# TensorE in the emitted order: alternating heads, feed-forward by column budget, maxima by halves

## The chip, the cores and the metric

One core of one Trainium2 chip runs the whole program. The metric is device time in microseconds (us) of one execution. Below, PE is TensorE (matmuls), PEld its weight loads, DVE is VectorE, ACT is ScalarE, POOL is GpSimd, and SP issues most of the DMAs.

## The reference, cut to what matters

Attention whose queries and keys are hashed to six bits, and which counts a key only where both hashes agree; then a gated feed-forward block over the heads' joined outputs. Four batches, eight heads, 768 rows, 64 columns a head.

```python
mask = q_bucket[:, :, :, None] == k_bucket[:, :, None, :]
scores = np.where(mask, scale * np.matmul(q, k.transpose(0, 1, 3, 2)), -1e9)
attn = np.exp(scores - np.max(scores, axis=-1, keepdims=True))
x = np.matmul(attn / (np.sum(attn, axis=-1, keepdims=True) + 1e-09), v)   # heads side by side: 512
u, w = np.split(np.maximum(x @ w_in, 0.0), 2, axis=-1)                    # 1024 wide
w = (w - mean(w)) / np.sqrt(var(w) + 1e-06)
out = (u * (np.einsum('ts,bsd->btd', w_spatial, w) + b_spatial[None, :, None])) @ w_out
```

## The kernel before, in words

Two heads make a pair: head 0 lies on partitions 0 to 63, head 1 on 64 to 127. There are 16 pairs, four a batch, and the rows are taken 128 at a time, so the attention has 96 steps; step g is row tile i = g % 6 of pair p = g // 6.

**A step.** `scores` (L269) fills one PSUM tile of two banks for each head (pool `ps_sc`, two tiles in all), by `sums` (L221): four passes of products, each as two column halves of 384 for each of the two heads, 16 matmuls. Operands are fp16 numbers split in a high and a low part, and the last pass adds the mask. The program's loops name the two heads in turn: `for a in passes, for c in halves, for e in heads`. A head's matmul uses only its 64 (or 63) rows of the array.

For most pairs, DVE then takes each row's extreme from the score tile (L285), ACT the exponential (L286) and a cast to fp16 (L293), DVE or POOL the low part (L294), and one transposing DMA on SP's queue turns the result (`pt<-pp`, L296). Three steps later (`LAG`) `weighted` multiplies it with V, 18 matmuls for each head (L309 to L311, "pv").

For pairs 1, 2 and 3 (`KEYS`) keys stand on the rows, so nothing needs to be turned: ACT takes the exponential (L277), and one step later 6 fp32 matmuls for each head follow (L266). These pairs need the rows' maxima beforehand: `row_max` (L236) makes a row tile's sums again, 8 matmuls, into two tiles of `ps_sc`, and DVE reduces them (L243). After six row tiles the maxima go to one line (a transpose on PE, L254, and a small DMA to `hk`).

**The feed-forward block.** When a batch's four pairs are done, 28 units stand in a queue: `v_unit`, `u_unit`, `s_unit`, `o_unit`, each 12 or 18 matmuls of 384 or 512 columns into one bank of `ps_m` (two banks, used by hashes and mean rows too). They run beside the next batch's attention; the last batch's run at the end, a part of them beforehand (`partial_units`).

**What sets the order.** `at(g, k)` gives each instruction a priority. A scheduler, which holds a model of the engines, places the instructions of all engines by it and by when it thinks their inputs are there. It so decides PE's order too: which head's matmul is next, where a unit falls between the scores of a step. Each engine then works off its list. Units are dropped into the program by whole units, `credit += 28.0 / STEPS` a step.

Also beside the first batch, `weights_gen` (L103) turns the feed-forward weights from 64 bits to fp16 pairs, 36 jobs; those of `w_in` and `w_out` have four DVE instructions each (L138 to L141).

Of the kernel before, what the change touches and what calls it, by code (L numbers as in the profile page):

```python
# [36 lines left out]
def lsh_attention_spatial_gating(  # L37
# [183 lines left out]
    def sums(p, ps, rows, passes, queries):  # L221

        for a, (x, y, last) in enumerate(passes):
            for c in range(2):
                cs = slice(c * HS, (c + 1) * HS)
                for e in range(2):
# [3 lines left out]
                    nc.tensor.matmul(ps[e][:, c], lhsT=f(l)[:, rows], rhs=f(m)[:, cs],  # L230
# [5 lines left out]
    def row_max(p, i):  # L236
        ps = [ps_sc.tile([P, 2, 512], F32, tag="sc", name=f"mp{p}_{i}_{e}")[:, :, :HS] for e in range(2)]
        sums(p, ps, slice(i * P, (i + 1) * P), ALL[2:], (True, True))
        for e in range(2):
            n = 2 * p + e  # L240
            if i == 0:
                st["mx", n] = wk.tile([P, NT], F32, tag="mx", bufs=3, name=f"mx{n}")
            nc.vector.reduce_max(st["mx", n][:, i:i + 1], ps[e], axis=AX.XY)  # L243
        if i < NT - 1:
            return
        for e in range(2):
            n = 2 * p + e
            nb = st["nb", n] = wk.tile([P, NT], F32, tag="nb", bufs=6, name=f"nb{n}")
            mx = st.pop(("mx", n))
            m16 = wk.tile([P, NT], F16, tag="m16", bufs=2, name=f"m16_{n}")  # L250
            nc.vector.tensor_scalar(m16, mx, -float(2 ** 27), -1.0 / HK, op0=ALU.max, op1=ALU.mult)
            nc.gpsimd.tensor_scalar(nb, mx, -ISQ, None, op0=ALU.mult)
            tp = ps_m.tile([P, 512], F32, tag=MT, name=f"tp{n}").bitcast(F16)
            nc.tensor.transpose(out=tp[0:NT, 0:P], in_=m16, identity=ident)  # L254
# [90 lines left out]
    def partial_units():  # L345
# [7 lines left out]
        def unit(name, lhs, rhs, dst):  # L353
            ps = ps_m.tile([P, 512], F32, tag=MT, name=name)[:, :dst.shape[-1]]
            k = 0
            for c in range(NPAIR - 1):
                for t in THREE:
                    nc.tensor.matmul(ps, lhsT=lhs(c, t), rhs=rhs(c, t), start=(k == 0), stop=(k == 3 * NPAIR - 4))  # L358
                    k += 1
            nc.scalar.copy(dst, ps)  # L360

        def v_part(i):
            flat = vb[i // 3].rearrange("p a s -> p (a s)").bitcast(F32)
            dst = st["vpart", i] = flat[:, (i % 3) * F2:(i % 3 + 1) * F2]
            unit(f"vpp{i}", lambda c, t: xt[c][:, t[0], i * P:(i + 1) * P], lambda c, t: wi[t[1]][:, c, F2:DF], dst)

        def u_part(d):
            dst = st["upart", d] = ub[:, d]
            unit(f"upp{d}", lambda c, t: wi[t[0]][:, c, d * P:(d + 1) * P], lambda c, t: xt[c][:, t[1], 0:HS], dst)
# [3 lines left out]
    def mlp_units(b):  # L373
# [14 lines left out]
        def v_unit(i):  # L388
# [3 lines left out]
            for c in range(k0 // 3, NPAIR):  # L392
                for gx, gw in THREE:
                    nc.tensor.matmul(ps, lhsT=xt[c][:, gx, i * P:(i + 1) * P], rhs=wi[gw][:, c, F2:DF],  # L394
# [12 lines left out]
            if i % 3 == 2:  # L407
                norm(i // 3)

# [20 lines left out]
        def u_unit(d, h):  # L430
# [10 lines left out]
            for c in range(k0 // 3, NPAIR):  # L441
                for gw, gx in THREE:
                    nc.tensor.matmul(ps[:, :HS], lhsT=wi[gw][:, c, d * P:(d + 1) * P], rhs=xt[c][:, gx, hs],  # L443
# [6 lines left out]
            nc.scalar.activation(u[h][:, d], ps, AF.Relu, scale=1.0 / SX)  # L450

        gt = {}

        def s_unit(d, h):
# [5 lines left out]
            for c in range(NT):  # L460
                for gv, gw in THREE:
                    nc.tensor.matmul(ps[:, :HS], lhsT=vn[gv][:, c, d * P:(d + 1) * P], rhs=ws[gw][:, c, hs],  # L462
# [6 lines left out]
            nc.gpsimd.tensor_tensor(out=gt[h][1][:, d], in0=y, in1=gt[h][0][:, d], op=ALU.subtract)  # L469

        def o_unit(i):
# [3 lines left out]
            for c in range(NF):  # L475
                for gg, gw in THREE:
                    nc.tensor.matmul(ps, lhsT=gt[h][gg][:, c, j * P:(j + 1) * P], rhs=wo[gw][:, c, :],  # L477
# [4 lines left out]
            nc.sync.dma_start(out=out[b, i * P:(i + 1) * P, :], in_=o)  # L482

# [34 lines left out]
    G_W = 0  # L518
    G_U = 1
    STEPS = NPAIR * NT  # L520
    LASTB = (NP - NPAIR) * NT + LAG
    LRATE = 1.48
    HQS = (nc.sync, nc.scalar, nc.gpsimd)
# [4 lines left out]

    at(-40, 0)
# [8 lines left out]
    queue = []  # L538
    wdone = 0
    credit = 0.0  # L540
    wv = 0
    rml = [(NT * p + i - LEAD, p, i) for p in sorted(KEYS) for i in range(NT)]
# [109 lines left out]
```

## Time and profile before

| | us |
|---|---|
| median of 3 runs (lowest, highest) | 897.3 (890.99, 898.1) |
| the profiled execution | 894.64 |
| its span, first to last instruction | 892.9 |
| PE busy in it | 829.5 |
| DVE, ACT, POOL busy | 528.1, 445.9, 308.0 |

The profile is of one execution. Busy time is the union of an engine's instructions; overlapping matmuls count once. In the view by stretches, "PEclk" is the share of full clock that the profiler recorded as granted; its first record in this execution lies at about 265 us.

### The profile page before, as it was taken

To read this page: it belongs to the slowest core of one execution; us is meant where nothing else is said; L and a number is where in the kernel's file an instruction comes from. 1 tells how busy PE (TensorE), PEld (TensorE's weight loads), DVE (VectorE), ACT (ScalarE), POOL (GpSimd) and SP (SyncE) were. 2 spreads that over 40 slices of the span, in tenths; PEclk is the share of its full clock that TensorE was granted. 3 is DMA by queue.
4 is the path that set the end of the run, shared out by engine and by line. 5 is a ranking of instruction groups with operands and counts; after the bars stand their busy time and mean duration, and the time that the engine had idled before them with its cause. 6 is when DMAs were issued, how large, how long until landed. Compare 5 with 4: busy or idle time off the path is not lost. (4 is left out here: it accounts for less than half of the span.)

```text
span 892.9 us, 16563 instructions
## 1 busy us (share of the span) xinstructions
PE 829.5 (93%) x6622; PEld 474.9 (53%) x6622; DVE 528.1 (59%) x963; ACT 445.9 (50%) x684; POOL 308.0 (34%) x328
## 2 busy tenths in 40 slices
PE   3998899999999789988999999989998999999997
PEld 0344555566567345545555455546554556655554
DVE  5667581311123668985777797767685877674510
ACT  3244452211224576764666766565565756654522
POOL 6023331110021254654272334432451355252143
PEclk9999999999999889898999998999999999999999
DMA  4444730100020696978889879787969587977001
GB/s 130 104 102 114 181 104 1 57 18 1 1 72 14 125 217 127 184 136 171 152 157 176 167 134 172 117 190 126 184 118 211 98 162 131 163 127 131 18 1 72
DMA packets 290694, 104.15 MB, mean 117 GB/s; under 512 B 277560, under 2 KB 280632, under 8 KB 290616
## 3 DMA queue, kind: packets, MB, share of 16 engines
q1 hardware_dynamic: 290480, 103.04, 58.1%
q8 instruction: 52, 0.85, 0.4%
q14 instruction: 26, 0.21, 0.1%
q10 hardware_dynamic: 72, 0.03, 0.0%
q0 software_dynamic: 64, 0.02, 0.0%
HBM read 27.94 MB, written 6.29 MB: 38 GB/s over the span
## 5 line engine op out<-in xcount | busy, mean ns | idle before, releaser
L230 PE MATMUL sp<-hl 64*128 64x384 f16 x1152 | 222.4, 374 | 14.4 <-ACT ex L286 12.4
L286 ACT ACTIVATE ex<-sp,nb 128x768 f32<-128x768 f32 x156 | 138.1, 897 | 89.6 <-DVE ex L285 88.7
L285 DVE TENSOR_SCALAR_CACHE_REDUCE ex<-sp 128x768 bf16<-128x768 f32 x156 | 145.7, 951 | 47.9 <-PE sp L230 47.5
L294 DVE TENSOR_TENSOR pp<-ex,pp 128x768 f16<-128x768 f32 x120 | 126.7, 1068 | 71.0 <-ACT pp L293 70.7
L230 PEld LDWEIGHTS <-hl 64*128 64x128 f16 x1224 | 93.3, 104 | 117.0 <-issue 75.3
L293 ACT CAST pp<-ex 128x768 f16<-128x768 f32 x156 | 125.7, 831 | 4.7 <-DMA pt<-pp 3.1
L294 POOL TENSOR_TENSOR pp<-ex,pp 128x768 f16<-128x768 f32 x36 | 62.0, 1721 | 170.6 <-ACT pp L293 170.2
L309 PE MATMUL pv<-vp,pt 128*128 128x65 f16 x936 | 110.7, 200 | 6.1 <-DMA pt<-pp 5.9
L309 PEld LDWEIGHTS <-pt 128*128 128x128 f16 x936 | 90.3, 102 | 37.1 <-issue 22.0
L310 PE MATMUL pv<-vp,pt 128*128 128x64 f16 x936 | 109.9, 199 | 0.0
L311 PE MATMUL pv<-vp,pt 128*128 128x65 f16 x936 | 109.7, 201 | 0.0
L230 PE MATMUL sp<-hk 63*128 63x384 f16 (+1 forms) x384 | 99.4, 376 | 0.0
L462 PE MATMUL sps<-ws,vn 128*128 128x384 f16 x576 | 99.0, 327 | 0.0
L311 PEld LDWEIGHTS <-pt 128*128 128x128 f16 x936 | 91.0, 101 | 12.6 <-issue 11.8
L310 PEld LDWEIGHTS <-pt 128*128 128x128 f16 x936 | 91.0, 101 | 9.7 <-issue 6.0
L266 PEld LDWEIGHTS pv<-vf,ex 128*128 128x128 f32 x432 | 82.7, 290 | 25.2 <-issue 24.0
L266 PE MATMUL pv<-vf,ex 128*128 128x65 f32 x432 | 89.6, 383 | 2.7 <-DVE x L327 2.7
L328 POOL TENSOR_TENSOR x<-x,xf 128x384 f32<-128x384 f32 x31 | 35.8, 1153 | 150.6 <-DVE x L327 140.4
L462 PEld LDWEIGHTS <-vn 128*128 128x128 f16 x576 | 55.2, 98 | 36.7 <-issue 2.4
L277 ACT ACTIVATE ex<-sp 128x768 f32<-128x768 f32 x36 | 28.3, 804 | 89.0 <-PE sp L230 89.0
L477 PE MATMUL ops<-wo,g 128*128 128x512 f16 x288 | 68.3, 384 | 3.9 <-ACT g L468 3.2
L230 PEld LDWEIGHTS <-hk 63*128 63x128 f16 (+1 forms) x456 | 46.2, 114 | 44.8 <-issue 30.1
(95 smaller groups left out, 1025.7 us busy)
## 6 DMA issues: line engine op xcount, KB each, us to landing
qk<-kq SPq DMA_DIRECT2D x16, 768.0 KB
out<-o SPq DMA_DIRECT2D x24, 256.0 KB
v<-v SPq DMA_DIRECT2D x13, 384.0 KB
raw<-w_in SPq DMA_DIRECT2D x16, 256.0 KB
pt<-pp SPq DMA_TRANSPOSE x156
raw<-w_sp SPq DMA_DIRECT2D x12, 192.0 KB
raw<-w_out SPq DMA_DIRECT2D x8, 256.0 KB
hk<-sg SPq DMA_DIRECT2D x123, 9.0 KB
```

Source lines behind the costliest of these rows:

```text
L230: nc.tensor.matmul(ps[e][:, c], lhsT=f(l)[:, rows], rhs=f(m)[:, cs], start=(a == 0), stop=(a == len(passes) - 1))
L266: nc.tensor.matmul(acc[:, qi, :], lhsT=ex[:, qi * P:(qi + 1) * P], rhs=vf[p % 2][:, 2 * i + e, :], start=(i == 0 and qi == 0), stop=(i == ...
L285: nc.vector.tensor_scalar(jk, ps[e], -ISQ, None, op0=ALU.mult, op1=ALU.min, accum_out=nb)
L286: nc.scalar.activation(ex, ps[e], AF.Exp, bias=nb, scale=ISQ)
L293: nc.scalar.copy(pp[:, 0], ex)
L294: (nc.gpsimd if (e, i) in (PL_POOL if n >= 2 * NH else PL_POOL1) else nc.vector).tensor_tensor(out=pp[:, 1], in0=ex, in1=pp[:, 0], op=ALU. ...
L309: nc.tensor.matmul(acc, lhsT=pt[:, c, :], rhs=vh, start=(i == 0 and c == 0), stop=False)
L310: nc.tensor.matmul(acc[:, 0:D], lhsT=pt[:, c, :], rhs=vl, start=False, stop=False)
L311: nc.tensor.matmul(acc, lhsT=pt[:, NT + c, :], rhs=vh, start=False, stop=(i == NT - 1 and c == NT - 1))
L328: (nc.vector if n == 2 * NP - 1 else nc.gpsimd).tensor_add(x, x, f)
L462: nc.tensor.matmul(ps[:, :HS], lhsT=vn[gv][:, c, d * P:(d + 1) * P], rhs=ws[gw][:, c, hs], start=(k == 0), stop=(k == 3 * NT - 1))
L477: nc.tensor.matmul(ps, lhsT=gt[h][gg][:, c, j * P:(j + 1) * P], rhs=wo[gw][:, c, :], start=(k == 0), stop=(k == 3 * NF - 1))
```

## The change: what it does

1. `steps()` runs under a mode in which PE's instructions stand in the order in which the program emits them. The scheduler still places the other engines.
2. So the 16 score matmuls of a step alternate between the two heads and nothing stands between them.
3. The feed-forward units become generators that yield after each matmul; `fill` takes matmuls until a budget of columns is spent: 7000 a step, in two halves, 8200 in the last batch. A unit may be cut anywhere. A batch's units begin two steps later than they did (`WAIT`).
4. A step is then: scores, half a budget, maxima of one half, `weighted` of head 0, half a budget, maxima of the other half, `weighted` of head 1, then the hashes and mean rows.
5. Maxima are made by halves of 384 columns, both heads at a time, in the two banks of `ps_m` instead of the score tiles; DVE reduces 72 tiles of 384 columns instead of 36 of 768. The first pair's begin at step 2 instead of step 0. The scaling of the maxima moves from POOL to DVE.
6. The first eight hash rows are issued on two queues (SP, ACT) instead of three.

```diff
-    def row_max(p, i):
-        ps = [ps_sc.tile([P, 2, 512], F32, tag="sc", name=f"mp{p}_{i}_{e}")[:, :, :HS] for e in range(2)]
-        sums(p, ps, slice(i * P, (i + 1) * P), ALL[2:], (True, True))
+    def row_max(p, i, c):
+        ps = [ps_m.tile([P, 512], F32, tag=MT, name=f"mp{p}_{i}_{c}_{e}")[:, :HS].unsqueeze(1) for e in range(2)]
+        sums(p, ps, slice(i * P, (i + 1) * P), ALL[2:], (True, True), (c,))
...
+    def fill(g, columns):
...
+        credit[0] += columns
+        while credit[0] > 0:
+            if not running:
+                if not queue:
+                    credit[0] = 0.0
+                    return
+                running.append(queue.pop(0)())
+            at(g, G_F)
+            n = next(running[0], None)
+            if n is None:
+                running.clear()
+            else:
+                credit[0] -= n
...
+        rml = [(max(NT * p + i - LEAD, 2 + i // 2), p, i) for p in sorted(KEYS) for i in range(NT)]
...
+            rate = (RATE if g < LASTB else LRATE) / 2
+            for e in range(2):
+                fill(g, rate)
+                at(g, 100)
+                for r, j in now:
+                    row_max(r, j, e)
+                    if j == NT - 1 and e == 1:
+                        max_row(r)
+                at(g, 20)
+                v = wv
+                while v < NP * NT and v + (LAGK if v // NT in KEYS else LAG) <= g:
+                    m, j = divmod(v, NT)
+                    v += 1
+                    weighted(2 * m + e, j)
...
+    with tc.manual_schedule(engines={ET.PE}):
+        steps()
```

**PE, scores of step 27** (`sp4_3_0` and `sp4_3_1` are the two heads' tiles, `hl4` and `hk1` their operands, `pv` the product with V). Before:

```order
L230 LDWEIGHTS hk1_83
L230 MATMUL sp4_3_0_2152<-hk1_83 128x384
L309 LDWEIGHTS pt9_0_1926
L309 MATMUL pv9_2214<-vp0_94,pt9_0_1926 128x65
L310 LDWEIGHTS pt9_0_1926
L310 MATMUL pv9_2214<-vp0_94,pt9_0_1926 128x64
L311 LDWEIGHTS pt9_0_1926
L311 MATMUL pv9_2214<-vp0_94,pt9_0_1926 128x65
L230 LDWEIGHTS hl4_1372
L230 MATMUL sp4_3_1_2153<-hl4_1372 128x384
```

Now:

```order
L230 LDWEIGHTS hk1_83
L230 MATMUL sp4_3_0_2182<-hk1_83 128x384
L230 LDWEIGHTS hk1_83
L230 MATMUL sp4_3_1_2183<-hk1_83 128x384
L404 LDWEIGHTS xt0_1002
L404 MATMUL vps0_1_2170<-wi0_102,xt0_1002 128x512
```

Before, eight matmuls of head 0 stood in a row, then three of another kind, then eight of head 1. Now 16 stand in turn, and a feed-forward unit begun in the step before goes on behind them. Over the program the runs of score and maxima matmuls were 175, 108 of them in steps 27 to 94; now they are 110, one run of scores in each of the 96 steps and 14 of maxima apart from them.

**PE, maxima of pair 3 in the first batch** (`mp3_4`: row tile 4; `pv4` is L266's product with V). Before:

```order
L230 MATMUL mp3_4_0_1360<-hk0_82 128x384
L266 MATMUL pv4_1313<-vf0_98,ex4_2_1356 128x65 x6
L230 LDWEIGHTS hl3_878
L230 MATMUL mp3_4_1_1361<-hl3_878 128x384
L230 LDWEIGHTS hl3_878
```

Now:

```order
L230 MATMUL mp3_4_0_0_1430<-hl3_1017 128x384
L230 LDWEIGHTS hl3_1017
L230 MATMUL mp3_4_0_1_1431<-hl3_1017 128x384
L230 LDWEIGHTS hk0_82
L230 MATMUL mp3_4_0_0_1430<-hk0_82 128x384
L230 LDWEIGHTS hk0_82
L230 MATMUL mp3_4_0_1_1431<-hk0_82 128x384
L271 MATMUL pv4_1358<-vf0_98,ex4_1_1346 128x65 x6
```

Head 0's four matmuls for a row tile were followed by six products and then by head 1's four; now the four of one half alternate between the heads, and the first such group stands right behind the step's 16 scores.

**SP, the first loads** (`qk2` is the third pair's operands, `hk1` the second pair's hash rows). Before:

```order
L184 DMA hk1_83<-sg1_1_182 12x384 x8
L296 DMA_TRANSPOSE pt0_0_166<-pp0_0_163 128x12x128
L296 DMA_TRANSPOSE pt1_0_171<-pp1_0_168 128x12x128
L151 DMA qk2_196<-kq 128x1536
L296 DMA_TRANSPOSE pt0_1_264<-pp0_1_261 128x12x128
```

Now:

```order
L151 DMA qk2_198<-kq 128x1536
L301 DMA_TRANSPOSE pt0_0_168<-pp0_0_165 128x12x128
L301 DMA_TRANSPOSE pt1_0_173<-pp1_0_170 128x12x128
L184 DMA hk1_83<-sg1_1_184 12x384 x8
L301 DMA_TRANSPOSE pt0_1_228<-pp0_1_225 128x12x128
```

The load of the third pair moved ahead of the second pair's eight hash rows, which only the maxima and the second pair's scores read.

## Rows read from the trace of the kernel before

**Rows 1.** The page: span; busy us, share of span, instructions by engine.

```profile
span 892.9 us, 16563 instructions
PE 829.5 (93%) x6622; PEld 474.9 (53%) x6622; DVE 528.1 (59%) x963; ACT 445.9 (50%) x684; POOL 308.0 (34%) x328
```

**Rows 2.** By stretches: length; busy (count) of PE, PEld, DVE, ACT, POOL; PEclk; DMA share; GB/s.

```profile
0.00:129.30 129.30, 107.12 (x554) 53.87 (x555) 84.00 (x150) 53.65 (x91) 40.86 (x59) 1.00 0.49 124
129.30:281.40 152.10, 151.76 (x664) 95.50 (x664) 33.04 (x57) 33.83 (x47) 17.30 (x27) 1.00 0.09 25
281.40:305.44 24.04, 17.84 (x132) 8.85 (x131) 15.86 (x31) 11.97 (x18) 8.21 (x8) 0.86 0.47 92
305.44:810.07 504.63, 477.56 (x4746) 275.11 (x4743) 369.18 (x667) 318.27 (x476) 216.34 (x208) 0.96 0.83 155
810.07:892.90 82.83, 75.23 (x535) 41.58 (x532) 26.00 (x61) 28.16 (x54) 25.30 (x28) 1.00 0.20 47
```

**Rows 3.** By stretches again: step 18 of the 96, score block to score block.

```profile
241.74:252.58 10.84, 10.84 (x41) 7.29 (x41) 1.13 (x5) 1.72 (x3) 1.05 (x2) 1.00 0.00 0
```

**Rows 4.** By stretches, L230 alone (scores, maxima): length; PE, PEld busy; PEclk; DMA.

```profile
198.34:210.76 12.42, 6.93 (x24) 2.49 (x25) 1.00 0.00 1
268.44:272.67 4.23, 1.48 (x18) 0.70 (x18) 1.00 0.05 13
305.44:810.07 504.63, 168.25 (x1088) 78.73 (x1088) 0.96 0.83 155
```

**Rows 5.** Timeline of PE: start, us, engine, line, operation, out<-in, shape, count, idle before.

```profile
9.79 1.47 PE L230 MATMUL sp<-hl 64*128 64x384 f16 x8 [0.84 <-DVE hl L193]
...
207.47 0.82 PE L230 MATMUL mp<-hl 64*128 64x384 f16 x2
208.86 1.97 PE L266 MATMUL pv<-vf,ex 128*128 128x65 f32 x8
...
262.94 2.10 PE L230 MATMUL sp<-hl 64*128 64x384 f16 x12
...
268.44 1.15 PE L230 MATMUL sp<-hl 64*128 64x384 f16 x12
269.84 2.89 PE L266 MATMUL pv<-vf,ex 128*128 128x65 f32 x24
...
297.40 1.46 PE L394 MATMUL vps<-wi,xt 128*128 128x512 f16 x3 [5.17 <-DMA xt<-xs]
...
305.32 0.20 PE L311 MATMUL pv<-vp,pt 128*128 128x65 f16 x1
305.44 1.15 PE L230 MATMUL sp<-hl 64*128 64x384 f16 x6
306.85 0.20 PE L309 MATMUL pv<-vp,pt 128*128 128x65 f16 x1
```

**Rows 6.** L230 in 262 to 282 us: count, duration in ns, smallest/median/largest.

```profile
L230 PE MATMUL sp<-hl x56: 322/323/524, 262.9 to 281.9; 64*128 64x384 f16 x56
```

**Rows 7.** Waits in 305.44 to 810.07: total us, times, longest.

```profile
ACT ex L286 <- DVE ex L285: 63.0, 45, 2.8
DVE ex L285 <- PE sp L230: 36.7, 38, 3.5
PE sp L230 <- ACT ex L286: 12.4, 10, 2.4
```

**Rows 8.** Groups in 305.44 to 810.07: count, busy us, mean ns; idle before, releaser.

```profile
L462 PE MATMUL sps<-ws,vn 128*128 128x384 f16 x432 | 75.1, 328 | 0.0
L174 PE MATMUL hp<-qk,hc 128*32 128x384 f32 x72 | 8.1, 523 | 2.8 <-DVE sy L466 2.8
L466 DVE SCALAR_TENSOR_TENSOR sy<-sps,bt 128x384 f32<-128x384 f32 x24 | 13.2, 550 | 4.9 <-PE sps L462 3.7 <-POOL sy L467 1.2
```

**Rows 9.** A group of DVE in 0 to 129.3, with its count, busy us and mean ns.

```profile
L243 DVE TENSOR_REDUCE mx<-mp 128x1 f32<-128x768 f32 x21 | 19.8, 953 | 7.3 <-PE mp L230 7.3
```

**Rows 10.** Timeline of DVE: the first reading of scores.

```profile
16.63 0.95 DVE L285 TENSOR_SCALAR_CACHE_REDUCE ex<-sp 128x768 bf16<-128x768 f32 x1
```

More of the change, by code (lines that the diff above doesn't have):

```diff
@@ L219, in mean_row, with sums @@
         st["fm", p] = fm
-    def sums(p, ps, rows, passes, queries):
+    def sums(p, ps, rows, passes, queries, halves=(0, 1)):
         for a, (x, y, last) in enumerate(passes):
-            for c in range(2):
+            for c in halves:
                 cs = slice(c * HS, (c + 1) * HS)
@@ L229, in sums, with max_row @@
                     l, m = (x, y) if queries[e] else (y, x)
[L230 removed]
+                    nc.tensor.matmul(ps[e][:, c - halves[0]], lhsT=f(l)[:, rows], rhs=f(m)[:, cs],
                                      start=(a == 0), stop=(a == len(passes) - 1))
     ALL = ((0, 1, False), (2, 3, False), (2, 1, False), (1, 0, True))
[L236 to L238 removed]
+    def row_max(p, i, c):
+        ps = [ps_m.tile([P, 512], F32, tag=MT, name=f"mp{p}_{i}_{c}_{e}")[:, :HS].unsqueeze(1) for e in range(2)]
+        sums(p, ps, slice(i * P, (i + 1) * P), ALL[2:], (True, True), (c,))
         for e in range(2):
[L240 to L245, printed above, removed]
+            if i == c == 0:
+                st["mx", 2 * p + e] = wk.tile([P, NT, 2], F32, tag="mx", bufs=4, name=f"mx{2 * p + e}")
+            nc.vector.reduce_max(st["mx", 2 * p + e][:, i, c:c + 1], ps[e], axis=AX.XY)
+    def max_row(p):
         for e in range(2):
@@ L408, in v_unit @@
                 norm(i // 3)
+            yield F2
         def norm(g):
@@ L527, in at @@
         tc.cur_priority = int(1000 * (g + 40) + k)
+    queue = []
+    coming = []
+    running = []
+    credit = [0.0]
+    def fill(g, columns):
+        for t, units in list(coming):
+            if t <= g:
+                coming.remove((t, units))
+                queue.extend(units)
+        credit[0] += columns
[11 more added lines that the diff above has]
+                credit[0] -= n
@@ new lines, in prepare @@
+    def prepare(p, i):
+        if i == 1 and p + 2 < NP:
+            hash_rows(p + 2)
+        if i == 2 and p + 2 < NP:
+            split_qk(p + 2)
+        if i == 3 and p + 3 < NP:
+            load_qk(p + 3)
+        if i == 2 and 0 < p < NP - 1:
+            load_vf(p + 1)
+        if i == 3 and p + 1 < NP:
+            split_v(p + 1)
+            mean_v(p + 1)
+        if i == 4 and p + 2 < NP:
+            load_v(p + 2)
+        if i == 5 and p + 1 < NP:
+            mean_row(p + 1)
+        if i == 1 and p == 0:
+            mean_v(0)
+        if i == 3 and p == 0:
+            mean_row(0)
@@ L529, in lsh_attention_spatial_gating @@
+    G_F = 60
+    WAIT = 2
+    RATE = 7000
+    LRATE = 8200
     at(-40, 0)
@@ L608, in lsh_attention_spatial_gating @@
-    for _ in wg:
-        pass
-    while queue:
-        queue.pop(0)()
+    with tc.manual_schedule(engines={ET.PE}):
+        steps()
 def kernel(**inputs):
```

151 lines of the change are left out of this document (71 added, 80 removed).

## The prediction, on record before the run

> **What bounds the kernel now.** I read the page, then busy time by stretches, then the timeline of PE where two stretches differ, then the waits. PE is busy for 829.5 of 892.9 us [rows 1], and in three of the five stretches for over 90% of the time, with DVE at 73% at most [rows 2]. So PE's list sets the pace, and the question is what its time consists of.
>
> The reader is to see two things in it. First, a score block takes twice as long where the heads don't alternate: at 305.44 eight matmuls of one head last until 306.85, 1.41 us with the change to the next kind, and the other head's eight follow later; at 268.44 all 16 are over in 1.40 us [rows 5]. In step 21 the scores hold PE for 1.48 us; in 305.44 to 810.07 they hold it for 168.25 us, 2.47 a step over 68 steps [rows 4]. Pairs overlap; a run of one head doesn't.
>
> Second, the first batch runs at TensorE's lower level. Score matmuls there take 524 ns, and 322 or 323 afterwards [rows 6]; step 18, of scores and the product with V, takes 10.84 us [rows 3], and step 21, the same work, 4.23 [rows 4]. The column of granted clock says 1.00 in both, but its first record lies at about 265 us, so I go by the durations: 1.2 GHz before, 2.4 after. PE was busy all through step 18 [rows 3]. What came just before the rise is a block of scores at 262.94 in which the two heads alternated from first to last; the only one before it is step 0's, which waits for loads interrupt [rows 5]. Busy time with half the rows at work had not raised the clock in 250 us.
>
> **The change part by part**, against the profiled execution (894.64, which is 1.74 over its span and 0.3% under the median of 897.3).
>
> *Steps 27 to 94, now 504.63 us, 7.42 a step* [rows 2]. Alternating heads: 2.47 becomes 1.48, -0.99 a step [rows 4]. Fewer changes between score and other matmuls: one run costs about 0.2 us beside its matmuls (0.12 from the last product with V at 305.32 to the first score, and 1.41 us for eight scores, which are 8 x 0.16 at 384 columns and 2.4 GHz, so 0.1 behind them [rows 5]); 108 runs become 68, 40 x 0.2 / 68 = -0.12. The lower clock: a mean of 0.96 is 8% of 505 us at half speed, 40 us, in which 20 us are lost, -0.30 a step; scores there wait up to 2.4 us for exponentials and then run unpaired [rows 7], and I take it that pairs keep the clock up as they do from step 20 on. Left: 6.01.
>
> At 6.01 DVE's work, 369.18 / 68 = 5.43 a step, fills 90%; ACT's is 4.68; the DMAs' share of 0.83 is 6.2 us of a step, but they lie three steps ahead of their reader [rows 2]. PE idles 27 us there now, 0.40 a step. With its order fixed it will idle more, since the next scores need both tiles free, so both exponentials done, and DVE's list carries the low parts in between. I double the idle time: **6.4 a step**. Ends: 6.0 (nothing added) and 7.2 (DVE at 75%, about as full as now). 68 x 6.4 = 435; 28 feed-forward matmuls more than before are left for the end (403 against 375 in the two orders), 28 x 0.174 [rows 8] = 4.9: 430.
>
> *Steps 9 to 23, now 152.10* [rows 2]. At the upper level a step without maxima is 4.23 [rows 4]. Maxima add two groups of four matmuls. A group between products took 1.39 us (207.47 to 208.86 [rows 5]) unpaired and at the lower level; half of that is 0.70, its best pairing 0.4. Two groups are thus 0.8 to 1.4, I take 1.1 and 0.3 for the wait on the banks, which DVE must empty before the second group: 5.6. 7 x 5.6 + 8 x 4.23 = 73. Hashes and mean rows: 3 (eight records of a hash are 0.9 [rows 8]). Until the clock rises I allow three steps at the lower level, 10 us in all. Sum 86, which is -66. That is the largest uncertain term: at the lower level all through, step 14 would be 12.42 less half of its 6.93 of scores and maxima, less two changes: 8.6 [rows 4]; step 18 likewise 7.9 [rows 3]; the sum is 60 + 63 + 6 = 129.
>
> *Steps 0 to 8, now 129.3.* DVE works 84.0 us of it [rows 2]. The reductions of halves: 21 of 953 ns [rows 9] become 42 of about 550, the nearest row that reads 384 columns of PSUM [rows 8]: +3. The first scores need the loads; DVE reads them at 16.63 [rows 10], with some 10 us of its work done. So no less than 17 + 77 = 94, and not over 129 unless PE is worse placed than now. The second and third row tile's scores no longer wait behind maxima, and the third pair's load goes ahead of eight hash rows; but each group of maxima now waits for DVE, 2 x 0.55. I take 115, rather to the upper end for that wait: -14. Two queues instead of three for eight small rows: within 1 us. The scaling moved to DVE is six short instructions; nothing.
>
> *Steps 24 to 26, now 24.04,* with 6.2 of PE idle [rows 2] for the fourth pair's turned output. That chain of DVE, POOL, ACT and DMA stays: step 24 begins at 281.40, its products end 4.2 later, and the waiting unit goes on at 297.40 [rows 5], 12 us behind them. With 4.2 before it and a unit's rest of 1 behind it, 17. The two steps of delay for a batch's units lie in it.
>
> *The end, now 82.83,* plus the 4.9 from above: 88.
>
> Sum: 115 + 86 + 17 + 430 + 88 = 736; with 1.74 around the span, **738 us**.
>
> **A rule against it.** The Trainium skill, page "TensorE: Matmul & The Clock Gate", section "What's actually happening", says that the clock is throttled by default and that activity releases it. Read as busy time, it does not agree with the stretch 129.30 to 281.40, where PE was busy for 151.76 of 152.10 us [rows 2] and mostly slow. By that reading a kernel with more idle PE has less reason to rise, and the first batch would stay slow; that is the second rival, and the time would be its 781.
>
> **The rivals.**
> - *Evacuation takes over.* DVE must read both heads' score tiles before the second exponential frees them. For it: DVE at 5.43 a step, with its list set by a model. Against: DVE waited 36.7 us for scores, while scores waited 12.4 for exponentials [rows 7]. Steps of 7.2: 738 + 54 = 792. The Trainium skill, page "TensorEngine Tiling (Array Packing)", section "PSUM Bottleneck", says that packing speeds up TensorE but not the emptying of PSUM; the trace of before has no stretch that shows it.
> - *The clock stays down in the first batch*: 129 instead of 86: 781. For it: 250 us of it now. Against: the rise behind the first pairs.
> - *Everything pairs and nothing waits*: 6.0 a step, first steps at DVE's pace (105): 738 - 27 - 10 = 701.
> - *Slower than before.* PE now can't fill a wait: each step has two products with V whose operands come by one queue of transposing DMAs, and the scores behind them wait too. The other four stretches make 306, so it is slower from (893 - 306) / 68 = 8.6 us a step. DMA time is 6.2 of 7.42 [rows 2]; it would have to grow by 40%, or two chains follow each other in each step. At 9 a step: 920.
> - *It doesn't alternate after all*: excluded by the order, which shows pairs.
>
> **How the numbers follow.** Forecast 0.52 (713 to 765, the ends of steps 0 to 8 and half those of the steps), evacuation 0.15, clock 0.14, no waits 0.14, slower 0.03, no change by some mishap 0.02. The range is 690 to 805: it takes in the three rivals below 805 and the upper end of the step. Faster by over 1% (about what can be told from no change here) 0.95, within 1% 0.02, slower 0.03.
>
> **What would show it.** Right: L230 at about 1.5 us a step after 300 us; matmuls of 322 ns from about step 10; steps 9 to 23 in 80 to 95 us; 6.0 to 6.8 us a step in the three later batches, with PE still the busiest. Wrong: 524 ns until 200 us (the clock); PE idle over 1.2 us a step, released by ACT's exponentials (evacuation) or by `pt<-pp` (the DMAs).

## The result, and the profile after

The changed kernel takes **864.15 us** (median of 4 runs, 861.48 to 868.83) against 895.35 us for the kernel before in the same series (890.99 to 898.1): a ratio of 0.966, 95% interval 0.959 to 0.973. It is faster by 3.4%; 738 us were forecast, with a range of 690 to 805, so the prediction is wrong in size by 126 us. The profiled execution took 868.83 us, 1.83 over its span of 867.0. Of the experiments below, e2 and e8 had two and three executions in a slower state (without them their medians are 887.6 and 890.1 us), and e2's only profile is of such an execution, so its trace is not read.

The page of the changed kernel: span; busy time by engine; then PE's busy tenths in 40 slices.

```profile
span 867.0 us, 16611 instructions
PE 692.6 (80%) x6622; PEld 406.4 (47%) x6622; DVE 536.5 (62%) x1011; ACT 439.6 (51%) x684; POOL 317.7 (37%) x320
...
PE   3645569899588779697768878798879898989897
```

PE has 137 us less busy time than before [rows 1], and the span is only 26 us shorter: 111 us have turned into idle time. PE is nowhere full for more than two slices running.

The same five stretches as [rows 2], cut at the same score blocks (steps 0 to 8, 9 to 23, 24 to 26, 27 to 94, the end); columns as there.

```profile
0.00:133.89 133.89, 74.42 (x535) 37.52 (x536) 86.25 (x179) 56.05 (x97) 42.60 (x58) 0.76 0.47 121
133.89:222.22 88.33, 82.58 (x683) 60.78 (x683) 31.50 (x75) 29.93 (x40) 13.92 (x20) 0.90 0.15 41
222.22:245.44 23.22, 14.39 (x95) 7.79 (x95) 15.93 (x29) 12.08 (x18) 8.77 (x9) 0.78 0.51 95
245.44:775.46 530.02, 439.26 (x4751) 256.60 (x4751) 376.16 (x668) 311.08 (x474) 225.54 (x207) 0.90 0.75 147
775.46:867.00 91.54, 82.00 (x566) 43.74 (x563) 26.65 (x62) 30.44 (x58) 26.88 (x28) 0.99 0.20 48
```

| steps | before | forecast | after |
|---|---|---|---|
| 0 to 8 | 129.3 | 115 | 133.9 |
| 9 to 23 | 152.1 | 86 | 88.3 |
| 24 to 26 | 24.0 | 17 | 23.2 |
| 27 to 94 | 504.6 | 430 | 530.0 |
| end | 82.8 | 88 | 91.5 |

Steps 9 to 23, most of the first batch, came out at the size forecast and are the whole gain. Steps 27 to 94 became *slower*, 7.79 us a step instead of 7.42, though L230 there takes 1.82 us a step instead of 2.47 [rows 4]:

```profile
245.44:775.46 530.02, 123.83 (x1089) 57.49 (x1090) 0.90 0.75 147
```

What PE waits for in that stretch (total us, times, longest; `sp` are scores, `ops` output units, `pv` products with V, `mp` mean rows, `g` is the gate, `x` a head's output); before, the first kind was 12.4 us [rows 7] and all idle of PE 27 us [rows 2], now 91:

```profile
PE sp L230 <- ACT ex L291: 32.6, 26, 4.4
PE ops L496 <- ACT g L484: 11.6, 4, 6.6
PE pv L314 <- DVE x L332: 8.1, 4, 3.2
PE mp L216 <- ACT vr L411: 5.8, 3, 2.7
PE mp L216 <- DVE sy L482: 5.5, 1, 5.5
PE mp L216 <- ACT o L500: 5.5, 1, 5.5
```

One of these waits, in step 65, from three timelines: ACT, SP's queue, and PE (start, us, engine, line, operation, out<-in, shapes, count, idle before).

```profile
546.10 0.83 ACT L298 CAST pp<-ex 128x768 f16<-128x768 f32 x1
552.49 1.48 ACT L191 ACTIVATE hl<-qk 128x1536 f16<-128x1536 f32 x1 [5.55 <-DMA qk<-kq]
553.88 1.68 ACT L291 ACTIVATE ex<-sp,nb 128x768 f32<-128x768 f32 x2
555.45 0.59 ACT L500 ACTIVATE o<-ops 128x512 f32<-128x512 f32 x1
```

```profile
547.03 0.58 SPq L151 DMA_DIRECT2D qk<-kq  x1
```

```profile
556.18 0.77 PE L216 MATMUL mp<-vc,ones 128*128 128x128 f32 x2 [5.46 <-ACT o L500]
```

ACT's list holds the split of a later pair (L191) ahead of this step's exponentials. Its load was issued at 547.03, just as ACT came to it, and ACT waited 5.55 us; so exponentials and the emptying of a feed-forward bank stood still, and PE's list, at a matmul that needs that bank, with them. In all of steps 27 to 94, from the waits of ACT (11.2 us in 6 times in the kernel before):

```profile
ACT hl L191 <- DMA qk<-kq: 36.4, 8, 6.7
```

And what follows such an idle, in busy time by stretches:

```profile
540.90:554.60 13.70, 9.48 (x114) 5.49 (x111) 6.47 (x12) 5.83 (x7) 5.03 (x7) 1.00 1.02 203
554.60:561.40 6.80, 5.21 (x23) 2.28 (x24) 4.80 (x7) 3.81 (x7) 0.00 (x0) 0.50 0.82 201
```

PE stops at 550.7, and from 554.6 to 561.4 it has half the clock. By the clock records of the trace there are 17 such stretches in steps 27 to 94, 102 us in all, and ahead of each lies an idle of PE of 1.8 to 6.6 us; one idle of 2.2 us had none behind it. The kernel before has the same pattern in its steps 27 to 94: seven such stretches, 41 us in all, each behind an idle of PE of 1.7 to 3.6 us. One of them, behind an idle of 2.0 us that ended at 326.5:

```profile
327.00:333.80 6.80, 6.80 (x40) 3.26 (x39) 4.19 (x7) 6.80 (x13) 5.49 (x5) 0.50 0.91 231
```

### The profile page after: what moved, and what is told of

Same layout as the page of the kernel before. It is cut to its first block, busy times and chain, and to the rows that moved or that the text cites. A ratio compares the mean times of both kernels' runs of the same rounds, so it can differ in the third digit from the quotient of the medians.

```text
span 867.0 us, 16611 instructions
## 1 busy us (share of the span) xinstructions
PE 692.6 (80%) x6622; PEld 406.4 (47%) x6622; DVE 536.5 (62%) x1011; ACT 439.6 (51%) x684; POOL 317.7 (37%) x320
## 5 line engine op out<-in xcount | busy, mean ns | idle before, releaser
L299 DVE TENSOR_TENSOR pp<-ex,pp 128x768 f16<-128x768 f32 x120 | 132.5, 1123 | 77.7 <-ACT pp L298 77.5
L230 PE MATMUL sp<-hl 64*128 64x384 f16 x1152 | 143.3, 375 | 45.7 <-ACT ex L291 43.0
L290 DVE TENSOR_SCALAR_CACHE_REDUCE ex<-sp 128x768 bf16<-128x768 f32 x156 | 142.8, 951 | 36.7 <-PE sp L230 36.4
L230 PEld LDWEIGHTS <-hl 64*128 64x128 f16 x1224 | 66.4, 104 | 153.5 <-issue 121.3
L478 PE MATMUL sps<-ws,vn 128*128 128x384 f16 x576 | 107.5, 336 | 6.4 <-ACT u L463 3.4
L314 PEld LDWEIGHTS <-pt 128*128 128x128 f16 x936 | 90.8, 101 | 32.9 <-issue 21.2
L496 PE MATMUL ops<-wo,g 128*128 128x512 f16 x288 | 74.7, 398 | 19.6 <-ACT g L484 12.4
L456 PE MATMUL ups<-xt,wi 128*128 128x384 f16 x348 | 66.6, 336 | 5.5 <-ACT u L463 4.4
L271 PE MATMUL pv<-vf,ex 128*128 128x65 f32 x432 | 60.6, 299 | 6.9 <-DVE x L332 6.9
L230 PE MATMUL sp<-hk 63*128 63x384 f16 (+1 forms) x384 | 60.6, 366 | 4.8 <-DMA hk<-sg 4.8
L271 PEld LDWEIGHTS pv<-vf,ex 128*128 128x128 f32 x432 | 56.8, 213 | 15.2 <-issue 15.1
L483 POOL TENSOR_TENSOR sy<-sy,u 128x384 f32<-128x384 f32 x32 | 35.5, 1108 | 73.2 <-DVE sy L482 65.0
```

Of the source, the lines that this page charges most:

```text
L230: nc.tensor.matmul(ps[e][:, c - halves[0]], lhsT=f(l)[:, rows], rhs=f(m)[:, cs], start=(a == 0), stop=(a == len(passes) - 1))
L271: nc.tensor.matmul(acc[:, qi, :], lhsT=ex[:, qi * P:(qi + 1) * P], rhs=vf[p % 2][:, 2 * i + e, :], start=(i == 0 and qi == 0), stop=(i == ...
L290: nc.vector.tensor_scalar(jk, ps[e], -ISQ, None, op0=ALU.mult, op1=ALU.min, accum_out=nb)
L299: (nc.gpsimd if (e, i) in (PL_POOL if n >= 2 * NH else PL_POOL1) else nc.vector).tensor_tensor(out=pp[:, 1], in0=ex, in1=pp[:, 0], op=ALU. ...
L314: nc.tensor.matmul(acc, lhsT=pt[:, c, :], rhs=vh, start=(i == 0 and c == 0), stop=False)
```

## Experiments

Medians of 4 to 10 runs; the idle of PE and the mean granted clock are those of steps 27 to 94 in each profile (length less PE's busy time).

| | what differs | us | steps 27 to 94 | idle | clock |
|---|---|---|---|---|---|
| before | | 895.4 | 504.6 | 27.1 | 0.96 |
| changed | | 864.2 | 530.0 | 90.8 | 0.90 |
| e1 | late split moved | 843.2 | 509.8 | 82.5 | 0.93 |
| e2 | heads in turn | 888.5 | | | |
| e3 | before, one score tile | 1001.5 | 640.1 | 157.0 | 0.84 |
| e4 | weights later | 867.2 | 531.2 | 94.9 | 0.91 |
| e5 | e1, product banks first | 843.3 | 511.2 | 81.9 | 0.92 |
| e6 | e5, order and rate of units | 839.8 | 499.3 | 73.4 | 0.91 |
| e7 | half low parts | 853.9 | 514.8 | 82.9 | 0.92 |
| e8 | e5, heads in turn | 890.9 | 548.0 | 54.8 | 0.91 |
| e9 | e1, DVE's work spread | 838.5 | 505.5 | 73.1 | 0.93 |
| e10 | e9, order and rate of units | 835.5 | 494.4 | 73.8 | 0.95 |
| e11 | e10, more low parts on POOL | 830.9 | 485.2 | 61.1 | 0.94 |
| e12 | half minima | 852.7 | 513.6 | 87.1 | 0.93 |
| e13 | 46 us more for PE | 875.7 | 536.1 | 68.3 | 0.94 |
| e14 | e11, half low parts and minima | 813.0 | 476.4 | 60.0 | 0.94 |
| e15 | e11, six low parts on POOL | 828.8 | 485.4 | 66.1 | 0.95 |
| e16 | whole units | 845.7 | 504.0 | 73.9 | 0.93 |
| e17 | e1 and e16 | 831.8 | 496.8 | 70.3 | 0.92 |
| e18 | e11 and e16 | 827.4 | 492.0 | 67.4 | 0.93 |

One caution for all: the scheduler makes the lists of DVE, ACT, POOL and SP anew for every kernel. Between the traces of the changed kernel and of e7, e12 or e16, at least 50, 61 and 115 of DVE's some 850 operations stand elsewhere, so a difference of a few us is not the edit's alone. The runs come from several series, in which the median of the kernel before lay between 891.5 and 895.4 us; by the ratios to it, the gains of e1 and e16 over the changed kernel are 20 and 15 us instead of 21 and 18.

### e1: the late split

```diff
-            nc.scalar.activation(ex, ps[e], AF.Exp, bias=nb, scale=ISQ)
+            st["xi"] = nc.scalar.activation(ex, ps[e], AF.Exp, bias=nb, scale=ISQ).ins
...
-            split_qk(p + 2)
+            with tc.issue_after(st["xi"]):
+                split_qk(p + 2)
```

> The changed kernel with one edit: ScalarE's split of the pair after next is queued behind the exponentials of the step in which it is emitted, four steps further on, so that ScalarE's list no longer meets it some 5.5 us before its load has landed. Theory A (PE's fixed list has nothing else to do while ScalarE's list stands at a late load): the idle of PE once per pair (5.5, 4.4, 6.6, 3.4, 5.5, 2.8, 2.7 us at steps 35 to 77, about 31 us) goes, and with it the half-clock stretches behind it (some 3 us each): 820 to 840 us against 864. Rival B (the idle comes from the pairs themselves, which need both score tiles free at once): those stalls are taken over by the next wait for exponentials; 855 to 868 us.

843.2 us: 21 under the changed kernel (ratio to before 0.944, 0.941 to 0.947). The time lies just above theory A's range (820 to 840) and well below B's (855 to 868). ACT no longer waits for that load in steps 27 to 94; the stretch is 20 us shorter. But the idle fell by only 8 us, where A expected some 31; the rest came through the clock, 0.90 to 0.93. What PE waits for now:

```profile
PE sp L230 <- ACT ex L291: 31.0, 20, 5.7
PE pv L314 <- DVE x L332: 19.6, 5, 5.2
PE ops L496 <- ACT g L484: 7.9, 4, 2.9
```

The products now wait for their banks, 19.6 us instead of 8.1. The next kind of late operation has come up, as B said of exponentials.

### e2 and e8: heads in turn

```diff
-    def sums(p, ps, rows, passes, queries, halves=(0, 1)):
+    def sums(p, ps, rows, passes, queries, halves=(0, 1), only=None):
+        if only is None:
+            for e in range(2):
+                sums(p, ps, rows, passes, queries, halves, (e,))
+            return
...
-                for e in range(2):
+                for e in only:
                     r = slice(D * e, D * e + D - (last and queries[e]))
```

> The changed kernel with one edit: all score (and maxima) matmuls of the first head of a pair, then all of the second; everything else of PE's list stays. Prices the alternation. Theory A (alternation is worth what it seemed to be, the loss lies elsewhere): scores go from 1.49 to about 2.26 us a step, +52 us over steps 27 to 94, of which idle PE absorbs at most a third; and if pairs are what raises the clock in the first batch, steps 9 to 23 go from 88 to about 130 us. 920 to 960 us. If the clock there rises without pairs: about 890. Rival B (pairs cause the idle of PE, by needing both tiles at once): the idle of steps 27 to 94 falls from 91 to about 30 us and the time stays at 850 to 875.

> The kernel of e5 with the heads in turn instead of alternating (the edit of e2). In e2 alternation was worth 24 us, of which some 20 in the first batch. Theory A2: with the waits gone PE's work counts again, so alternation is worth 45 to 70 us here. Rival D: still 20 to 30 us.

e2: 888.5 us, so alternation is worth 24 us in the changed kernel: less than theory A's 56 to 96, more than B's nothing, and what A gave (about 890) for a clock that rises without pairs. On e5 it is worth 47.6 (890.9 against 843.3), within A2's range. That some 20 of e2's 24 us lie in the first batch, as e8's expectation has it, is not shown. By stretches, L230 alone and then all engines, in e8 (where the line is L233):

```profile
133.60:225.93 92.33, 42.70 (x297) 20.54 (x297) 0.92 0.17 44
248.51:796.53 548.02, 177.11 (x1088) 85.29 (x1089) 0.91 0.74 142
...
248.51:796.53 548.02, 493.19 (x4750) 285.71 (x4750) 378.24 (x670) 322.63 (x476) 224.52 (x208) 0.91 0.74 142
```

and in e5:

```profile
132.60:220.47 87.87, 33.41 (x297) 14.48 (x298) 0.89 0.19 50
242.55:753.76 511.21, 121.54 (x1088) 56.38 (x1088) 0.92 0.79 152
...
242.55:753.76 511.21, 429.35 (x4750) 252.36 (x4749) 379.04 (x671) 315.71 (x476) 230.73 (x207) 0.92 0.79 152
```

Three readings. Alternating takes 56 us from L230 in steps 27 to 94 and 64 from PE's busy time, and the stretch becomes 37 shorter: 27 us come back as idle (54.8 to 81.9). And steps 9 to 23 take 92.3 us with heads *in turn*, at a clock of 0.92: the alternation is not what raises the clock in the first batch. A third, against the kernel before: with the heads in turn in both, steps 27 to 94 take 548.0 us in e8 and 504.6 before, with 54.8 and 27.1 us of idle. The emitted order, with the other edits that e8 has and the kernel before has not, loses 43 us there, and alternating then gains 37; which of these edits loses them was not separated.

### e3: alternation, with the scheduler's list

```diff
-        ps = [ps_sc.tile([P, 2, 512], F32, tag="sc", name=f"sp{p}_{i}_{e}")[:, :, :HS] for e in range(2)]
+        both = ps_sc.tile([P, 4, 512], F32, tag="sc", name=f"sp{p}_{i}")
+        ps = [both[:, 2 * e:2 * e + 2, :HS] for e in range(2)]
```

(and so for the maxima, with one buffer instead of two).

> The kernel before with one edit: the two heads' score tiles (and those of the maxima) are one tile of four banks, so that the scheduler can start neither head alone and puts out runs of 16 that alternate; PE's list is still the scheduler's. Alternation without the fixed list. Theory A: scores 1.49 us a step, PE idle in the three later batches stays near 30 us since the scheduler has other work to put in; the first batch rises to the upper clock early: 504 - 52 = 452, 152 becomes about 100, the other stretches as before: 780 to 810 us. Rival B (needing both tiles at once makes the idle): idle 80 to 100 us there, 840 to 880 us.

1001.5 us: neither theory. What PE waits for in steps 27 to 94:

```profile
PE pv L311 <- DMA pt<-pp: 117.7, 75, 6.1
PE sp L230 <- ACT ex L288: 17.1, 11, 3.6
```

It doesn't wait for exponentials, as B had it, but for the transposing DMAs: in the list that the scheduler made for this tile, the products stand before their operands land. So a list made at build time is not always safer than an emitted one, and "the scheduler has other work to put in" did not hold here: on the chip both lists are fixed. Steps 9 to 23 took 96.3 us at a clock of 0.95, so the clock rises there in the scheduler's order too.

### e4: the weights later

```diff
-    W_PTS = ((1, 0), (21, 16), (30, 28), (34, 37))
+    W_PTS = ((8, 0), (21, 16), (30, 28), (34, 37))
```

> The changed kernel with one edit: the preparation of the weights starts at step 9 instead of step 2, so that VectorE's list no longer holds a weight's conversion, which waits for its load, ahead of the maxima that free PE's banks. Theory A (the same mechanism as with the split: an operation on a late load ahead in an in-order list): steps 0 to 8 fall from 134 to 105 to 118 us, steps 9 to 23 gain at most 5: 838 to 855 us. Rival C (VectorE's work as such sets the pace of steps 0 to 23, wherever the weights stand): what steps 0 to 8 lose, steps 9 to 23 gain; 860 to 868.

867.2 us: no gain; rival C's time. Steps 0 to 8 and 9 to 23 in e4:

```profile
0.00:122.86 122.86, 77.92 (x534) 39.63 (x536) 83.05 (x167) 48.42 (x78) 37.06 (x51) 0.79 0.48 122
122.86:220.36 97.50, 89.34 (x683) 64.67 (x683) 36.66 (x88) 37.73 (x59) 19.69 (x27) 0.83 0.19 50
```

Eleven us are gained in the first stretch and nine given back in the second, at a lower clock (0.83 instead of 0.90). C's reason is not shown: DVE works 36.7 of the 97.5 us there.

### e5: the product banks emptied first

```diff
...
+                with ExitStack() as behind:
+                    if "xn" in st:
+                        behind.enter_context(tc.issue_after(st["xn"]))
+                    if p not in KEYS and g >= NT:
...
+                        turn(p, i)
...
+                    with tc.issue_after(st["tr"]):
+                        prepare(p, i)
```

(`xn` is the multiplication in `normalize` that reads the product bank.)

> The kernel of e1 with one more edit: in the step that ends a pair's products, VectorE's list has the four operations that empty the product banks in one piece, ahead of that step's low parts and of the next splits (in e1 the four are spread over 9.6 us, 510.2 to 519.8). Theory A2 (what is left of PE's idle stands at places where VectorE's and ScalarE's lists hold less urgent work ahead): the waits of the first product of a pair (3.3, 5.2, 1.8, 5.1, 1.1, 4.2, 3.1 us, 24 us in all) and the half clock behind each of them (about 3 us) go: 800 to 825 us against 843. Rival D (VectorE's work as such, 5.5 us a step beside 5.9 of PE, sets the pace): the low parts that are put off make the next scores late; 838 to 848 us.

843.3 us: rival D. DVE's timeline in e1 shows what was moved: L328, L329, L330 and L332 of one head, with other work between.

```profile
510.23 0.16 DVE L328 TENSOR_SCALAR rv<-pv 128x6 f32<-128x6 f32 x1
511.05 1.61 DVE L192 SCALAR_TENSOR_TENSOR hl<-qk,hl 128x768 f16<-128x768 f32 x1 [0.65 <-ACT hl L191]
512.58 1.58 DVE L193 SCALAR_TENSOR_TENSOR hl<-qk,hl 128x768 f16<-128x768 f32 x1
514.08 0.18 DVE L329 RECIPROCAL rv<-rv 128x6 f32<-128x6 f32 x1
514.18 2.51 DVE L299 TENSOR_TENSOR pp<-ex,pp 128x768 f16<-128x768 f32 x2
516.62 0.15 DVE L330 SCALAR_TENSOR_TENSOR rv<-nb,rv 128x6 f32<-128x6 f32 x1
...
519.79 0.54 DVE L332 TENSOR_TENSOR x<-pv,rv 128x384 f32<-128x384 f32 x1
```

In e5 this wait of the products is gone from the list of waits, and that of the scores has grown from 31.0 to 56.0 us:

```profile
PE sp L230 <- ACT ex L291: 56.0, 29, 6.0
```

### e6, e9, e10, e11, e15: spreading the work

e6 and e10 put the output units of a batch's first half behind the u units of the second, and take `RATE = 6400` instead of 7000. e9's core:

```diff
+        with tc.issue_after(st["xi"]), tc.issue_after(st["xd"]):
+            if i == 5 and N0 <= p + 2 < NP:
+                split_qk(p + 2, 0)
+            if i == 0 and N0 <= p + 1 < NP:
+                split_qk(p + 1, 1)
+            if i == 1 and N0 <= p < NP:
+                split_v(p)
+                mean_v(p)
...
+        if i == 4 and N0 <= p + 2 < NP:
+            hash_rows(p + 2)
```

e11 has `PL_POOL = ((1, 0), (1, 2), (1, 3), (1, 5))`, e15 all six rows of head 1 in both lists.

> The kernel of e5 with two edits more: the first half's output units stand behind the second half's u units, so that they do not wait for the gate just made, and 6400 columns a step instead of 7000, so that the feed-forward does not run dry two steps before the next batch. Theory A2: the waits of output units on the gate (4.5, 3.6, 3.9 us) and those of the dry steps 50 to 52 (9 us), with the half clock behind them, go, some 15 to 25 us under e5. Rival D: within 5 us of e5.

> The kernel of e1 with VectorE's work per pair spread over the six steps from pair 6 on: the second split in step 0, the split of V in step 1, emptying the product banks in 2, the rest of the output in 3, hashes in 4, the first split in 5, each queued behind the exponentials' minima of its step; in e1 some 8 us of these stand within two steps. Amounts of work, PE's list of scores, products and feed-forward are the same. Theory D2 (a burst in VectorE's list per pair, not its total, makes the waits of 3 to 6 us that moved from the products in e1 to the scores in e5): most of them go, with the half clock behind them: 805 to 828 us against 843. Rival E (VectorE's total of 5.5 us a step sets it, wherever it stands): 838 to 848.

> The kernel of e9 with the two edits of e6 (output units of the first half behind the second half's u units; 6400 columns a step). D2: 3 to 15 us under e9, since the waits on the gate and the dry steps go: 795 to 822 us. Rival E: within 4 us of e6's 840.

> The kernel of e10 with four instead of two of a pair's twelve low parts on GpSimd in the last two batches, as in the first two: about 2 x 1.1 us less on VectorE per pair, some 0.35 us a step. Rival E (total work of VectorE): 8 to 15 us under e10. D2: within 5 us of e10, either way (the operations of VectorE beside GpSimd's take up to 1.6 us instead of 0.95).

> The kernel of e11 with all six low parts of the second head of a pair on GpSimd, in all batches (four now). VectorE loses another 2.2 us a pair, some 0.37 us a step, GpSimd gains 3.6. If VectorE's time still counts and GpSimd's slower 1.8 us a part lie beside other work: 820 to 828 us against 831. If VectorE's operations slow down beside GpSimd's or the transfers wait for GpSimd: 830 to 840.

839.8, 838.5, 835.5, 830.9 and 828.8 us. e6 went by rival D (3.5 us under e5); e9 and e10, 5 and 3 us each, went by or close to rival E, far from D2's 805 to 828 and 795 to 822; e11's 5 us lie at the edge of D2's 5, and not in E's 8 to 15; e15's 2 us can't be told from none, and are neither of its cases. A burst spread out is worth little here.

### e7, e12, e14: less work for DVE

```diff
-            (nc.gpsimd if (e, i) in (PL_POOL if n >= 2 * NH else PL_POOL1) else nc.vector).tensor_tensor(out=pp[:, 1], in0=ex, in1=pp[:, 0], op=ALU.subtract)
...
+                nc.vector.tensor_tensor(out=pp[:, 1, 0], in0=ex[:, 0], in1=pp[:, 0, 0], op=ALU.subtract)
```

```diff
...
-            nc.vector.tensor_scalar(jk, ps[e], -ISQ, None, op0=ALU.mult, op1=ALU.min, accum_out=nb)
+            nc.vector.tensor_scalar(jk, ps[e][:, :, 0:HS:2], -ISQ, 3.0, op0=ALU.mult, op1=ALU.min, accum_out=nb)
```

> The changed kernel with less work on VectorE: its low parts are computed for half of the columns only (the other half of that part stays zero, so this half is left out of the result); PE's list, the other engines' work and the transfers stay. Takes about 0.5 us from each of 106 operations in steps 27 to 94, some 55 of VectorE's 376 us. Rival D (VectorE's work sets the pace there): 815 to 840 us against 864, nearly all that VectorE saves. Theory A (single late operations in the lists set it, the late load first): the stalls at the split stay; 850 to 864 us.

> The changed kernel with shorter minima on VectorE: they read every other column of a score tile (the scale is bounded so that nothing overflows), so the scale of a row is taken from half of its keys. About 0.4 us from each of two operations a step, in sum about what e7 takes from the low parts (e7: 864 to 854), but here on the chain from one step's scores to the next: scores, minimum, exponential, scores. Theory F (that chain, 4.6 us of a step at best, meets work queued ahead of it, so its length decides): 815 to 842 us. Rival E (VectorE's total): 848 to 858, as e7.

> The kernel of e11 with the cuts of e7 and e12 together (low parts on VectorE for half of the columns, the other half left out as zero; minima over every other column, the scale bounded): VectorE's work falls by about 1.4 us a step, after the late load, the burst and the dry steps are gone. Theory G (several causes in a row, each of which hides the next: with VectorE's work reduced alone the late load stands, with the late load moved VectorE stands): now nearly all of it shows; steps 27 to 94 fall from 485 to 440 to 460 us and the time from 831 to 785 to 808. Rival H (what is left of PE's idle stands at the feed-forward's own chain and banks): at most 15 us under e11, 815 or more.

e7 leaves out half of the low parts that DVE makes, e12 half of the columns in the minima. 853.9 and 852.7: 10 and 11 us for some 50 us of DVE's work each (48 and 57 of 376.2), alike whether or not the work lies on the chain from scores to scores. So D (815 to 840) and F (815 to 842) fell; the times lie in A's range (850 to 864) and E's (848 to 858). e14: 813.0, 18 under e11, of which 9 in steps 27 to 94, where PE still waits 60 us though DVE works only 274 of 476:

```profile
234.52:710.90 476.38, 416.35 (x4737) 246.41 (x4738) 273.51 (x656) 311.93 (x473) 228.16 (x221) 0.94 0.86 163
```

G (785 to 808) fell as well; H (815 or more) is nearer. DVE's amount of work is not what held the forecast's 6.4 a step off.

### e13: more work for PE

```diff
-                    nc.tensor.matmul(ps, lhsT=xt[c][:, gx, i * P:(i + 1) * P], rhs=wi[gw][:, c, F2:DF],
-                                     start=(k == k0), stop=(k == 3 * NPAIR - 1))
+                    for again in (0,) if k > k0 or last else (1, 1, 1, 0):
+                        nc.tensor.matmul(ps, lhsT=xt[c][:, gx, i * P:(i + 1) * P], rhs=wi[gw][:, c, F2:DF],
+                                         start=(k == k0), stop=(k == 3 * NPAIR - 1 or again > 0))
```

(and so in the other three kinds of unit.)

> The changed kernel with 252 matmuls more: the first one of each feed-forward unit of the first three batches is issued four times (each time from the start, so the result stays), 252 x 0.184 = 46 us of PE's work at the upper clock, nearly all in steps 27 to 94; no other engine gets work. If PE's own work sets the time there: 905 to 920 us against 864. Theory A/F (PE waits 91 us there, so its work has room): 868 to 885, and idle of PE falls by 25 us or more.

875.7 us; in steps 27 to 94:

```profile
250.03:786.08 536.05, 467.73 (x4993) 272.87 (x4993) 370.76 (x668) 313.94 (x474) 226.33 (x208) 0.94 0.76 145
```

The time lies in the range of A/F. Steps 27 to 94 take 6 us more for some 45 us of work: the idle fell by 22 us, and the clock rose to 0.94, which pays for most of the rest. PE's own work does not set the time there alone. This is the plainest evidence on why 44 us less of L230 [rows 4] do not show; that they are worth something all the same is what e2 says.

### e16, e17, e18: whole units

```diff
-        while credit[0] > 0:
+        while credit[0] > 0 or running:
```

> The changed kernel without the budgets: a feed-forward unit that has begun is put out whole (12 to 18 matmuls) before the products of its step, as the kernel before does it; same columns in the mean, heads still alternate, PE's list still the emitted one. If cutting the units by budgets kept the waits short: slower than 864 by 10 us or more, with more idle at the scores. If the waits come from single late operations and from the chain over VectorE and ScalarE, whichever way the units are cut: 856 to 872.

> The changed kernel with the edits of e1 (late split moved, -21 us) and e16 (whole units, -18 us) together. If the two stand at different places (ScalarE's list behind a late load; banks that a begun unit holds over scores and products): 820 to 830 us. If they hide each other: 838 to 846.

> The kernel of e11 (831 us) with whole units as in e16. If the banks held by begun units are what stood there after the late split, the burst and the dry steps were gone: 805 to 818 us, steps 27 to 94 at 455 to 470. If not: 826 to 836.

e16: 845.7 us, 18 *faster* than with budgets, where at best 8 were expected. Its waits of PE in steps 27 to 94:

```profile
PE sp L230 <- ACT ex L291: 42.3, 37, 4.1
PE pv L314 <- DVE x L332: 9.5, 4, 4.4
PE mp L216 <- ACT u L463: 7.1, 2, 5.5
...
PE ops L496 <- ACT g L484: 3.7, 2, 2.9
PE ops L496 <- POOL g L485: 1.9, 2, 1.0
```

The waits of the mean rows and hashes for a bank and of the output units for the gate are less than half of those of the changed kernel; those for exponentials are longer in sum. A unit that is cut keeps one of the two banks of `ps_m` over scores and products, which fits; that this is the cause was not isolated. e17 with both edits: 831.8, 32 of the 39 us that the two give singly, so they are mostly separate. e18 adds the rest: **827.4 us** (ratio to before 0.927, 0.923 to 0.931), not to be told from e15, and in the range given for the case that banks held by begun units are not what is left. Whole units are thus worth 18 us in the changed kernel, 11 in e1 and some 3 in e11: most of their gain is also had by e11's edits. These are the fastest that compute everything, 4% under the changed kernel.

## Why the prediction was wrong, point by point

- **Steps 27 to 94, the term that failed: "I double the idle time: 6.4 a step", with "I take it that pairs keep the clock up".** 100 of the 131 us between sum and profiled execution lie here. Idle: 90.8 us instead of 54 (+36). Clock: 102 us of the stretch are at the lower level; PE is busy for 81 of these, so about 41 us were lost where none were foreseen (+41). Work: the other 399 us instead of 376 (+23), of which only the double count below is traced. The step of the forecast that failed is treating idle and clock as separate, and idle as a modest extra: all idles of PE of 1.8 us or more, but one, have a slow stretch behind them. The trace of before had it already, with an idle ahead of each of its seven slow stretches; the forecast doubled the idle and in the same sum took the clock's loss off.
- **The price of alternating.** 2.47 to 1.48 was forecast; the scores took 1.82, since a fifth of the time was at half speed. The 2.47 of before held slow stretches too, which I then took off once more, as the -0.30 a step for the lower clock: part of it was counted twice.
- **Where the idle comes from.** Not PE's amount of work alone (e13), nor DVE's (e7, e12, e14). Operations that wait in the lists of ACT and DVE ahead of what PE needs: the split behind its load, 21 us (e1, shown); the cutting into budgets, 18 us (e16, shown as an effect, its path only likely, and mostly the same us as those of the next). Spreading, order, rate and POOL gave 12 more from e1 to e11, in small steps. The forecast listed DMAs as "three steps ahead of their reader"; that holds for the transposes, which PE does not wait for in this stretch. The load of q and k, whose split the scheduler puts so early in ACT's list that ACT comes to it as the load is issued, was missed.
- **The rivals.** "Evacuation takes over" at 7.2 a step named the largest wait, scores on exponentials, 32.6 of 91 us; the time was 7.79, between it and the 8.6 at which the change loses. The prediction's own sign of being wrong, idle of over 1.2 us a step, came true (1.33), but exponentials released only a third of it. None of the prices held the clock.
- **Steps 9 to 23: right in size (88.3 for 86), wrong in reason, so the size was luck.** "The rise behind the first pairs" is refuted by e8, where the clock rises with the heads in turn; in e3 it rises without the emitted order. The reading of the durations against the column was right: most other executions of the kernel before list a mean clock of 0.87 at the same time, where the profiled one has 0.97 for want of records. What kept the clock down for 265 us there, with PE busy throughout from 129 us on, stays open.
- **Steps 0 to 8: 133.9, above the upper bound of 129.** DVE's list held a weight's conversion ahead of scores and maxima, and that waited for ACT, which waited 15.13 us for a load (DVE, ACT, then the waits of PE in these steps):

```profile
42.20 0.08 DVE L290 DVE_READ_ACCUMULATOR ex<-sp 128x1 f32 x1
50.94 0.29 DVE L138 TENSOR_SCALAR w<-w 128x256 f32<-128x256 f32 x1 [8.65 <-ACT w L137]
50.48 0.43 ACT L137 ACTIVATE w<-raw 128x256 f32<-128x256 f32 x1 [15.13 <-DMA raw<-w_in]
PE mp L230 <- DVE mx L242: 33.6, 14, 10.8
```

  PE waited 33.6 us for DVE to empty the banks of the maxima, where the forecast had 2 x 0.55 a group; the longest of these waits, 10.8 us, is the one above, and what the others stand behind was not followed. I had counted DVE's work and looked at the loads of q and k alone. In e4, moving the weights away only moved the time.
- **Steps 24 to 26** (23.2 for 17): not the turned output of the fourth pair, as forecast, but the scores of step 26 wait, 8.5 us, for exponentials that stand in ACT's list behind a cast of the output (L338, 4.65 us of waiting for POOL) and a weight (L142, 1.86 us for its load), and whose minima stand in DVE's list behind that output's low part (L339). **The end** (91.5 for 88): size only.

```profile
237.32 0.48 PE L230 MATMUL sp<-hl 64*128 64x384 f16 x1 [8.52 <-ACT ex L291]
```

Still open: e18 takes 492 us for steps 27 to 94, 62 over the forecast. It idles 67 us there, 48 of them in 42 waits of the scores for exponentials, none longer than 3.9 us. No single cause of that rest was found, and 6.4 a step was not reached by any kernel (e14, which leaves work out, 7.0).

## What to carry to other kernels

When an engine's work is cut, ask next which in-order lists feed it, and read in each what stands ahead of the operation that it waits for; a load that lands later than one list assumes can stop all of them. Price each idle of PE with the half-clock stretch that follows it; the trace of the kernel before can show how often it does. Adding harmless work to the supposed bottleneck, as e13 does, is a cheap test of whether it is one, and could have been the first experiment; read the clock beside it, since the added work raised it here.

## What the runs showed of the hardware beyond expectation

In a kernel whose PE is busy 83% of steps 27 to 94 the clock fell 17 times, behind idles as short as 1.8 us; about 41 us were lost. The Trainium skill, page "TensorE: Matmul & The Clock Gate", section "HAM oscillation — how this bites in real kernels", describes waits in a loop that send the clock down each time; the trace agrees that waits do so, though the waits that it describes are longer than the shortest here.

DVE's elementwise operations stretch: L192 takes 0.96 us at best and 1.76 at most in steps 27 to 94 of e1, and the one above, 1.61, ran beside an operation of POOL (L325, 1.54 us from 511.80). The Trainium skill, page "SBUF — State Buffer", section "Summary: rules for kernel authors", says that of a DVE operation with two SBUF inputs and a GpSimd operation that reads SBUF, the second to issue waits for the first; the stretched durations would fit, but no run here separated it.
